# The order in which the first chunk's transfers are issued: next tiles of keys and values, weights and summaries in another sequence

## The chip, the cores and the metric

The kernel runs on one core of a Trainium2 chip. The metric is the device time of one execution in microseconds (us); the figure for the kernel before is the median of 3 runs. The trace comes from one further execution, taken by the hardware profiler. Its engines are TensorE (PE, with its weight loads as PEld), VectorE (DVE), ScalarE (ACT), GpSimd (POOL) and SyncE (SP); SP issues nearly all DMA transfers here.

## The reference

```
def _attn_ref(q, k, v):                      # batch 4, heads 8, sequence 768, head size 64
    block, window = (32, 16)
    k_sum = k.reshape(B, H, nb, block, D).max(axis=3)     # one maximum per 32 keys
    v_sum = v.reshape(B, H, nb, block, D).mean(axis=3)    # one mean per 32 values
    ...
    mask_l = np.abs(pos[:, None] - pos[None, :]) < window
    scores_s = scale * einsum(q, k_sum) + np.log(block)
    scores_all = np.concatenate([where(mask_l, scores_l, -1e9), scores_s], axis=-1)
    ...                                                   # softmax over both parts
    return np.matmul(a, np.concatenate([v, v_sum], axis=2))

def _moe_ref(x, w_in, w_out):                # x: 3072 x 512, w_in: 512 x 2048, w_out: 2048 x 512
    h = x @ w_in
    g = np.where(h > 0.0, h, exp(minimum(h, 0.0)) - 1.0)
    return g @ w_out
```

Each query attends to its neighbours in a window and to one summary per block of 32 (the maximum of the keys, the mean of the values). A feed-forward network with an ELU follows. The weights come as 64-bit floats.

## The kernel before

**Tiles.** The 3072 tokens are worked in 6 chunks of 512. In a chunk the network runs 16 steps, one for each 128 columns of the hidden layer: `layer1(c, f)` is 12 matmuls into a PSUM tile `h`, the ELU runs on ACT and DVE, `split` makes a high part `gh` (ACT) and a low part `gl` (POOL), and `layer2(c, f)` adds 12 matmuls into four accumulators one step later. Products are made in high and low parts, hence the pairs xh/xl and gh/gl.

**Attention beside it.** Attention for later tokens is cut into units: a third of a batch's sequence (256 queries) for one of four pairs of heads. Unit u is worked beside steps 2u and 2u+1. In step 2u TensorE makes the scores of unit u+1 (`unit_scores`, line 464), DVE finds their maxima (`unit_low`, line 130), ACT takes the exponentials, and TensorE makes the transposes of unit u (line 149); in step 2u+1 it makes the values of unit u (line 156), which ACT and DVE carry over to xh (line 169) and xl (line 170). The scores of unit u+1, the transposes and the values all use one PSUM bank, `a0`, in the first chunk.

**Loads of a unit.** `load_unit(u)` issues six transfers on SP (queries `qbd` in two, keys `kw` and values `vw` in a middle and an edge part): 64, 64, 144, 144, 40 and 40 KB.

**Summaries of the next batch.** `load_summary` brings 384 KB of keys or values of one pair of heads into a tile `n`, and `summary` reduces it on DVE (line 440). In the first chunk the tiles `n` lie in space that later belongs to weights (`spares`).

**Weights.** The 32 blocks of the two weight matrices, 512 KB each, come in the order (1,0), (1,1), (2,0), (1,2), (2,1), ..., where (1,f) is a block of w_in and (2,f) of w_out. `load_more(n)` issues loads until n blocks have been issued. `convert` turns a block into a high and a low part: POOL (line 103), ACT (108), DVE (110 and 113), ACT (117) and POOL (118). Two blocks are begun in every step of the first chunk, blocks number 4+2n and 5+2n in step n (counted from 0). The PSUM bank `a1` between ACT's line 108 and DVE's line 113 is one tile, so one conversion follows the other.

**Who sets the order.** The first chunk's instructions stand in the order in which the code is written, on all engines (`manual_schedule`); each engine works its queue in order. From the second chunk on only TensorE and SP are ordered by hand. Each DMA on SP also waits until the transfer eight before it has landed, since there are eight DMA semaphores in turn.

`first_units()` works the first 512 tokens' attention, converts the first blocks, and loads units 0 and 1; the loop `for n in range(NF)` with the 16 steps of the first chunk follows, and in each step `slot_a(n, 0)` makes unit scores and calls `load_unit(u + 2)` in even steps.

Of the kernel before, what the change touches and what calls it, by code (L numbers as in the profile page):

```python
# [17 lines left out]
F32 = mybir.dt.float32  # L18
# [8 lines left out]
P = 128  # L27
WIN = 16
E = WIN
BLK = 32  # L30
# [8 lines left out]
def attn_elu_ffn(ctx: ExitStack, tc: tile.TileContext, qT, kT, vT, v, w_in, w_out, out):  # L39
    nc = tc.nc  # L40
    B, NP, _, S = qT.shape
# [3 lines left out]
    NS = S // BLK  # L45
# [13 lines left out]
    att = ctx.enter_context(tc.tile_pool(name="att", bufs=2))  # L59
# [24 lines left out]
    def load(key):  # L84
        i, f = key
        if i == 1:
            load_weight(key, w_in[:, f * P:(f + 1) * P].rearrange("(c p) f -> p c f", p=P))
        else:
            load_weight(key, w_out[f * P:(f + 1) * P, :].rearrange("p (c f) -> p c f", c=1))

    def load_more(n):
        while loads and len(order) - len(loads) < n:
            load(loads.pop(0))
# [78 lines left out]
    def put_means(b, p, v_t, copy=None):  # L172
        src = vs_all[b][p * BLK:p * BLK + NS, :].rearrange("n (o d) -> n o d", o=1)
        (copy or nc.sync.dma_start)(out=v_t[KB:KC, :, :], in_=src.broadcast_to([NS, v_t.shape[1], P]))

    def put_maxima(b, p):
        nc.gpsimd.tensor_copy(out=kw[p][:, :, KB:KC], in_=ks_all[b][:, p:p + 1, :].broadcast_to([P, UW, NS]))

    def new_summaries(b):
        ks_all[b] = att.tile([P, NP, NS], F32, tag="ks", name="ks")  # L180
        vs_all[b] = att.tile([P, P], F32, tag="vs", name="vs", bufs=1)

    spares = {}

    def first_units():
# [74 lines left out]
        for p in range(NP):  # L260
            src = v[0, :, p * P:(p + 1) * P]
            whole = bass.AP(tensor=src.tensor, offset=src.offset + (QW - E) * row,
                            ap=[[row, KB], [QW * row, W2 - 1], [1, P]])
            nc.sync.dma_start(out=v_t[p][0:KB, 1:W2, :], in_=whole)
            nc.sync.dma_start(out=v_t[p][E:KB, 0, :], in_=src[0:KB - E, :])
        load_more(3)
        load_unit(0)
        load_more(6)
        load_unit(1)
        load_more(9)  # L270

        def maxima(p):
            nc.vector.tensor_reduce(out=ks[:, p, :], in_=kn[p][:, E:E + S].rearrange("p (n k) -> p n k", k=BLK),
# [107 lines left out]
        next(three)  # L381
        for p in range(NP):
            put_means(0, p, vw[p])
        load_more(12)
        return three


# [2 lines left out]
    def load_unit(u):  # L390
        third, p = units[u]
        b, th = divmod(third, NTH)
        q_t = qbd[u % 2]
        for h in range(2):
            nc.sync.dma_start(
                out=q_t[h * D:(h + 1) * D, :, h * D:(h + 1) * D],
                in_=qT[b, p, h * D:(h + 1) * D, th * UT:(th + 1) * UT].rearrange("d (t q) -> d t q", q=QW))
        lo = 1 if th == 0 else 0
        hi = UW - 1 if th == NTH - 1 else UW
        src = kT[b, p]  # L400
        nc.sync.dma_start(out=kw[p][:, lo:hi, 0:KB],
                          in_=bass.AP(tensor=src.tensor, offset=src.offset + (th * UW + lo) * QW - E,
                                      ap=[[S, P], [QW, hi - lo], [1, KB]]))
        vsrc = v[b, :, p * P:(p + 1) * P]
        nc.sync.dma_start(out=vw[p][0:KB, lo:hi, :],
                          in_=bass.AP(tensor=vsrc.tensor, offset=vsrc.offset + ((th * UW + lo) * QW - E) * row,
                                      ap=[[row, KB], [QW * row, hi - lo], [1, P]]))
        if th == 0:
            nc.sync.dma_start(out=kw[p][:, 0, E:KB], in_=src[:, 0:KB - E])
            nc.sync.dma_start(out=vw[p][E:KB, 0, :], in_=vsrc[0:KB - E, :])  # L410
            put_maxima(b, p)
        if th == NTH - 1:
            nc.sync.dma_start(out=kw[p][:, UW - 1, 0:KB - E], in_=src[:, S - KB + E:S])
            nc.sync.dma_start(out=vw[p][0:KB - E, UW - 1, :], in_=vsrc[S - KB + E:S, :])

    vst_all = {}

    def load_summary(b, p, src, spare=None):
        if p == 0 and src is kT:
            new_summaries(b)  # L420
            vst_all[b] = att.tile([P, NP, BLK], F32, tag="vst", name="vst", bufs=1)
            nc.gpsimd.memset(vst_all[b][:, :, NS:BLK], 0.0)
        parts = 1 if spare else 2
        m = NS // parts
        got = []
        for i in range(parts):
            if spare:
                n = wts.tile([P, m, BLK], F32, tag=spare, name="n")
            else:
                n = ffn.tile([P, m, BLK], F32, tag="cv", name="n", bufs=2)  # L430
            nc.sync.dma_start(out=n, in_=src[b, p, :, i * m * BLK:(i + 1) * m * BLK].rearrange("p (n k) -> p n k", k=BLK))
            got.append(n)
        return got

    def summary(b, p, src, got):

        dst, op = (ks_all[b], ALU.max) if src is kT else (vst_all[b], ALU.add)
        m = NS // len(got)
        for i, n in enumerate(got):
            nc.vector.tensor_reduce(out=dst[:, p, i * m:(i + 1) * m], in_=n, axis=AX.X, op=op)  # L440
# [32 lines left out]
    def unit_norm(u):  # L473
        normalize(sm_of[u], z_of.pop(u))
# [17 lines left out]
    def layer1(c, f):  # L492
        xh, xl = xs[c]
        w = weights[(1, f)]
        h_ps = psum.tile([P, CH], F32, tag="h", name="h", bufs=2)
        k = 0
        for cc in range(NCC):
            cols = slice(cc * P, (cc + 1) * P)
            for a, bb in ((0, xh), (0, xl), (1, xh)):
                nc.tensor.matmul(h_ps, w[:, a, cols], bb[:, cc, :], start=(k == 0), stop=(k == 3 * NCC - 1))  # L500
                k += 1
        return h_ps
# [78 lines left out]
    def begin_next():  # L581

        tile = convert() if todo else iter(())
        next(tile, None)
        return tile
# [4 lines left out]

    with tc.manual_schedule(engines=set(engines.values())):
        late = first_units()
        got = {}
        e = None
        this = begin_next()
        for n in range(NF):
            u, odd = divmod(n, 2)

            h_ps = layer1(0, n)
            next(this, None)  # L600
            ahead = begin_next()
            if n > 0:
                split(0, n - 1, e)
            next(this, None)
            if n > 0:
                evacuate()
            list(late)
            if not odd:
                unit_norm(u)
            for key in [(n - 1, 0), (n - 2, 1)]:  # L610
                if key in got:
                    summary(1, key[0], (kT, vT)[key[1]], got.pop(key))
            slot_a(n, 0)
            if n < NP:
                got[n, 0] = load_summary(1, n, kT, spares[0][n])
            if 1 <= n < NP + 1:
                got[n - 1, 1] = load_summary(1, n - 1, vT, spares[1][n - 1])
            load_more(12 + 3 * (n + 1))

            late, this = this, ahead  # L620
            next(this, None)
            ahead = begin_next()
            e = exp_of(h_ps)
            next(this, None)
            list(late)
            if not odd:
                low = unit_low(u + 1)
            elu(e, h_ps)
            if odd:
                unit_exps(u + 1, low)  # L630
            if n > 0:
                layer2(0, n - 1)
            late, this = this, ahead
            evacuate = slot_b(n, 0)
        list(late)
        split(0, NF - 1, e)
        evacuate()
        unit_norm(NF // 2)

    with tc.manual_schedule(engines={engines["PE"], engines["SP"]}):  # L640
        for n in range(NF, NCH * NF):
            c, f = divmod(n, NF)
            u, odd = divmod(n, 2)
            h_ps = layer1(c, f)
            e = exp_of(h_ps)
            turn = elu(e, h_ps)
            split(c, f, e)
            slot_a(n, c)
            if not odd and u + 1 < len(units):
                unit_exps(u + 1, unit_low(u + 1))  # L650
                unit_norm(u + 1)
            for b, first in first_of.items():
                p = n - (2 * first - 8)
                for q, src in ((p, kT), (p - 2, vT)):
                    if 0 <= q < NP:
                        got = load_summary(b, q, src)
                        with tc.issue_after(turn):
                            summary(b, q, src, got)
            layer2(*divmod(n - 1, NF))
            slot_b(n, c)()  # L660
        layer2(NCH - 1, NF - 1)
# [37 lines left out]
```

## Time and profile before

| what | value |
|---|---|
| median of 3 runs | 667.55 us (667.48 to 667.73) |
| the profiled execution | 666.64 us |
| its span, first to last instruction | 664.9 us |
| TensorE busy | 642.8 us, 97% of the span |
| VectorE, ScalarE, GpSimd busy | 265.3, 275.3, 244.1 us |
| DMA moved | 60.24 MB, mean 91 GB/s |

The span is the time from the first to the last instruction; the execution's own time holds 1.74 us more around it. Shares are means over the whole span, and the stages differ: DMA moves about 300 GB/s in the first sixth and little later. A row of a timeline gives start, duration, engine, line, operation and, in brackets, the idle time of the engine before it with what ended that.

### The profile page before, as it was taken

How to read it: one execution, taken by the hardware profiler on the slowest of the kernel's cores; microseconds unless marked ns; L12 is line 12 of the kernel's file. 1: busy time of each engine (PE TensorE's matmuls, PEld its weight loads, DVE VectorE, ACT ScalarE, POOL GpSimd, SP SyncE). 2: the span in 40 equal slices, each digit the busy share in tenths (PEclk: the TensorE clock that was granted, in tenths of full speed). 3: DMA queues.
4: the chain of work that ended last, by engine and by line, in shares of the span. 5: the costliest groups of instructions: out<-in, count | busy, mean ns of one | idle time of the engine just before them, and what ended most of it. 6: DMA issues, size and time to landing. Idle time of an engine off the chain costs nothing.

```text
span 664.9 us, 10778 instructions
## 1 busy us (share of the span) xinstructions
PE 642.8 (97%) x3916; PEld 525.1 (79%) x3916; DVE 265.3 (40%) x856; ACT 275.3 (41%) x750; POOL 244.1 (37%) x263
## 2 busy tenths in 40 slices
PE   8767899999999999999999999999999999999997
PEld 7655678888888887888888887888788888888885
DVE  7847877643323542323223452322332222322222
ACT  6754667653433344334333433433343333322222
POOL 5765789953232223222222322232223222222221
PEclk9977999999999999999999999999999999999999
DMA  9999981213132334112112552121312100100001
GB/s 317 253 287 328 333 260 42 67 33 96 39 79 57 112 92 118 51 32 60 36 32 55 162 142 52 44 62 33 96 40 53 32 1 1 63 1 1 0 1 63
DMA packets 86324, 60.24 MB, mean 91 GB/s; under 512 B 46464, under 2 KB 78464, under 8 KB 86272
## 3 DMA queue, kind: packets, MB, share of 16 engines
q1 hardware_dynamic: 82960, 53.66, 29.2%
q10 hardware_dynamic: 3312, 5.90, 2.4%
q8 instruction: 31, 0.51, 0.3%
q14 instruction: 21, 0.17, 0.1%
HBM read 52.46 MB, written 6.29 MB: 88 GB/s over the span
## 4 chain that ended last, share of the span: by engine, by line
PE 90%; DMA 6%; DVE 2%; SPq 1%; issue 1%; POOL 0%; ACT 0%; DVEq 0%; POOLq 0%
PE h L500 39%; PE o L528 38%; PE s L464 5%; PE o_ps L156 4%; DMA raw_w<-in_w_in_dram 3%; PE t_ps L149 3%; DMA raw_w<-in_w_out_dram 2%; PE s L287 1%; DMA vw<-in_v_dram 1%; DMA n<-in_vT_dram 1%; PE idle L224 1%; SPq L81 0%; DVE cv L113 0%; DVE sh L110 0%; DVE sm L130 0%
## 5 line engine op out<-in xcount | busy, mean ns | idle before, releaser
L500 PE MATMUL h<-xh,w 128*128 128x512 f32 x768 | 261.8, 402 | 0.0
L518 POOL TENSOR_TENSOR gl<-e,gh 128x512 fp32r<-128x512 f32 x96 | 123.5, 1287 | 217.4 <-issue 112.9
L528 PE MATMUL o<-w,gh 128*128 128x512 f32 x768 | 197.8, 396 | 0.0
L500 PEld LDWEIGHTS h<-xh,w 128*128 128x128 f32 x768 | 144.7, 189 | 31.0
L528 PEld LDWEIGHTS o<-w,gh 128*128 128x128 f32 x768 | 141.9, 189 | 28.6 <-issue 0.6
L500 PE MATMUL h<-xl,w 128*128 128x512 f32 x384 | 150.3, 391 | 0.0
L510 DVE TENSOR_SCALAR e<-e 128x512 f32<-128x512 f32 x96 | 43.7, 455 | 253.7 <-ACT e L506 253.6
L506 ACT ACTIVATE e<-h 128x512 f32<-128x512 f32 x96 | 57.3, 597 | 206.4 <-PE h L500 205.1
L144 POOL TENSOR_TENSOR sm<-sm,z 128x480 f32<-128x480 f32 x48 | 47.4, 987 | 158.1 <-ACT gh L517 141.9
L528 PE MATMUL o<-w,gl 128*128 128x512 f32 x384 | 105.4, 389 | 0.0
L517 ACT CAST gh<-e 128x512 fp32r<-128x512 f32 x96 | 59.0, 615 | 74.6 <-DVE e L511 73.3
L137 ACT ACTIVATE sm<-sm,mx 128x120 f32<-128x120 f32 x192 | 73.5, 385 | 26.6 <-DVE mx L130 26.6
L528 PEld LDWEIGHTS o<-w,gl 128*128 128x128 f32 x384 | 72.0, 188 | 15.2 <-POOL gl L518 0.2
L500 PEld LDWEIGHTS h<-xl,w 128*128 128x128 f32 x384 | 72.6, 189 | 12.8
L511 DVE SCALAR_TENSOR_TENSOR e<-h,e 128x512 f32<-128x512 f32 x96 | 66.2, 689 | 2.2
L464 PEld LDWEIGHTS s<-kw,qbd 128*128 128x128 f32 x320 | 43.1, 198 | 15.5 <-DVE xl L170 8.0
L464 PE MATMUL s<-kw,qbd 128*128 128x120 f32 x320 | 44.2, 283 | 11.2 <-DVE xl L170 6.7
L170 DVE TENSOR_TENSOR xl<-o_ps,xh 128x256 fp32r<-128x256 f32 x48 | 20.0, 422 | 61.3 <-ACT xh L169 61.3
L118 POOL TENSOR_TENSOR w<-cv,w 128x512 fp32r<-128x512 f32 x32 | 41.5, 1298 | 6.3 <-ACT w L117 5.5
L130 DVE CUSTOM_DVE_ANT_0 sm<-s,mask 128x120 f32<-128x120 f32 x192 | 42.2, 276 | 3.0 <-PE s L464 2.8
L137 ACT ACTIVATION_READ_ACCUMULATOR sm<-sm,mx 128x1 f32 x192 | 36.1, 188 | 0.0
L156 PEld LDWEIGHTS o_ps<-pt,vw 120*64 120x64 f32 x640 | 21.9, 137 | 14.1 <-ACT gh L517 9.2
(66 smaller groups left out, 369.3 us busy)
## 6 DMA issues: line engine op xcount, KB each, us to landing
raw_w<-in_w_in_dram SPq DMA_DIRECT2D x16, 512.0 KB, 4.5
raw_w<-in_w_out_dram SPq DMA_DIRECT2D x16, 512.0 KB, 9.4
qbd<-in_qT_dram SPq DMA_DIRECT2D x80, 64.0 KB, 2.3
out_dram<-ot ACTq DMA_DIRECT2D x20, 256.0 KB, 2.3
kw<-in_kT_dram SPq DMA_DIRECT2D x28, 144.0 KB
vw<-in_v_dram SPq DMA_DIRECT2D x28, 144.0 KB, 2.7
n<-in_kT_dram SPq DMA_DIRECT2D x16, 192.0 KB, 2.4
n<-in_vT_dram SPq DMA_DIRECT2D x16, 192.0 KB, 2.5
```

What stands on the lines that cost most here:

```text
L130: nc.vector.tensor_tensor_reduce(out=sm[:, t, :], in0=s_ps[:, t, :], in1=m, scale=-scale, scalar=3.0e38, op0=ALU.add, op1=ALU.min, accum_o ...
L137: nc.scalar.activation(out=sm[:, t, :], in_=sm[:, t, :], func=AF.Exp, bias=mx[:, t, :], scale=-1.0, accum_out=z[:, t, :])
L144: nc.gpsimd.tensor_tensor(out=sm, in0=sm, in1=z.broadcast_to([P, UW, KC]), op=ALU.mult)
L156: nc.tensor.matmul(o_ps[h * D:(h + 1) * D, t * QW:(t + 1) * QW], v_t[0:KC, w0 + t, h * D:(h + 1) * D], pt[0:KC, t, h * QW:(h + 1) * QW], s ...
L464: nc.tensor.matmul(s_of[u][:, t, :], qbd[u % 2][:, t, :], kw[p][:, t, :], start=True, stop=True)
L500: nc.tensor.matmul(h_ps, w[:, a, cols], bb[:, cc, :], start=(k == 0), stop=(k == 3 * NCC - 1))
L506: nc.scalar.activation(out=e, in_=h_ps, func=AF.Exp)
L510: nc.vector.tensor_scalar(out=e, in0=e, scalar1=1.0, scalar2=-1.0, op0=ALU.min, op1=ALU.add)
L511: top = nc.vector.scalar_tensor_tensor(out=e, in0=h_ps, scalar=0.0, in1=e, op0=ALU.max, op1=ALU.add)
L517: nc.scalar.copy(out=gh, in_=e)
L518: nc.gpsimd.tensor_tensor(out=gl, in0=e, in1=gh.bitcast(F32), op=ALU.subtract)
L528: nc.tensor.matmul(o_acc[c][s], a[:, s * P:(s + 1) * P], w[:, bb, :], start=first and f == 0, stop=last and f == NF - 1)
```

## The change

Three things are put in another order; no computation is added or taken away. In `first_units`, block (2,0) comes behind unit 0, and blocks (1,2) and (2,1) behind unit 1, where three blocks stood ahead of unit 0 and six ahead of unit 1; by the end of `first_units` 10 blocks are issued instead of 12. In step n the loads reach block count 12+2n instead of 12+3(n+1). The summaries follow a table `sums_at`: step number to a list of (0 for keys, 1 for values; pair of heads). A summary is loaded two steps before the step that reduces it, where it was loaded one step before (keys) or issued and reduced in neighbouring steps (values). New tiles for the summaries, and the memset of `vst`, move ahead of the loop.

```
-        load_more(3)
-        load_unit(0)
-        load_more(6)
+        load_more(2)
+        load_unit(0)
+        load_more(3)
         load_unit(1)
-        load_more(9)
+        load_more(5)
...
-        load_more(12)
+        load_more(10)
...
+        sums_at = {2: [(1, 0)], 3: [(0, 0)], 4: [(1, 1)], 5: [(0, 1), (1, 2)], 6: [(1, 3)], 7: [(0, 2)], 8: [(0, 3)]}
         got = {}
+        new_summaries(1)
...
-            for key in [(n - 1, 0), (n - 2, 1)]:
-                if key in got:
-                    summary(1, key[0], (kT, vT)[key[1]], got.pop(key))
+            for i, p in sums_at.get(n, []):
+                summary(1, p, (kT, vT)[i], got.pop((i, p)))
             slot_a(n, 0)
-            if n < NP:
-                got[n, 0] = load_summary(1, n, kT, spares[0][n])
-            if 1 <= n < NP + 1:
-                got[n - 1, 1] = load_summary(1, n - 1, vT, spares[1][n - 1])
-            load_more(12 + 3 * (n + 1))
+            for i, p in sums_at.get(n + 2, []):
+                got[i, p] = load_summary(1, p, (kT, vT)[i], spares[i][p])
+            load_more(12 + 2 * n)
```

On TensorE and ACT the sequence of instructions is the same before and after, and behind the first chunk it is the same on every engine. (A line that stands at 182 to 415 before stands 3 lines lower down in the change, and one from there to the loop stands 1 line higher up.)

SP, from the end of `first_units`, before: `raw_w_F_n<-in_w_in_dram` is block (1,F), `in_w_out_dram` block (2,F); `qbd_70`, `kw_72`, `vw_76` belong to unit 0 and `qbd_71`, `kw_73`, `vw_77` to unit 1.

```order
L81 DMA raw_w_0_181<-in_w_out_dram 128x512
L395 DMA qbd_70<-in_qT_dram 64x4x64 x2
L401 DMA kw_72<-in_kT_dram 128x3x96
L405 DMA vw_76<-in_v_dram 96x3x128
L413 DMA kw_72<-in_kT_dram 128x80
L414 DMA vw_76<-in_v_dram 80x128
L81 DMA raw_w_2_189<-in_w_in_dram 128x4x128
L81 DMA raw_w_1_191<-in_w_out_dram 128x512
L81 DMA raw_w_3_193<-in_w_in_dram 128x4x128
L395 DMA qbd_71<-in_qT_dram 64x4x64 x2
L401 DMA kw_73<-in_kT_dram 128x3x96
```

The same place of SP in the change:

```order
L398 DMA qbd_70<-in_qT_dram 64x4x64 x2
L404 DMA kw_72<-in_kT_dram 128x3x96
L408 DMA vw_76<-in_v_dram 96x3x128
L416 DMA kw_72<-in_kT_dram 128x80
L417 DMA vw_76<-in_v_dram 80x128
L81 DMA raw_w_0_187<-in_w_out_dram 128x512
L398 DMA qbd_71<-in_qT_dram 64x4x64 x2
L404 DMA kw_73<-in_kT_dram 128x3x96
L408 DMA vw_77<-in_v_dram 96x3x128
L416 DMA kw_73<-in_kT_dram 128x80
L417 DMA vw_77<-in_v_dram 80x128
L81 DMA raw_w_2_195<-in_w_in_dram 128x4x128
```

Block (2,0) moved behind unit 0, and blocks (1,2), (2,1) and (1,3) moved from ahead of unit 1 to behind it.

SP in steps 0 and 1, before, from the load of unit 2 (`qbd_70`, `kw_74`, `vw_78`) on; `n<-in_kT_dram` and `n<-in_vT_dram` are the summaries' loads:

```order
L395 DMA qbd_70<-in_qT_dram 64x4x64 x2
L401 DMA kw_74<-in_kT_dram 128x3x96
L405 DMA vw_78<-in_v_dram 96x3x128
L413 DMA kw_74<-in_kT_dram 128x80
L414 DMA vw_78<-in_v_dram 80x128
L431 DMA n<-in_kT_dram 128x768
L81 DMA raw_w_5_722<-in_w_out_dram 128x512
L81 DMA raw_w_7_724<-in_w_in_dram 128x4x128
L81 DMA raw_w_6_726<-in_w_out_dram 128x512
L431 DMA n<-in_kT_dram 128x768
L431 DMA n<-in_vT_dram 128x768
```

In the change:

```order
L398 DMA qbd_70<-in_qT_dram 64x4x64 x2
L404 DMA kw_74<-in_kT_dram 128x3x96
L408 DMA vw_78<-in_v_dram 96x3x128
L416 DMA kw_74<-in_kT_dram 128x80
L417 DMA vw_78<-in_v_dram 80x128
L430 DMA n<-in_vT_dram 128x768
L81 DMA raw_w_4_718<-in_w_out_dram 128x512
L81 DMA raw_w_6_720<-in_w_in_dram 128x4x128
L430 DMA n<-in_kT_dram 128x768
```

The first summary loaded is one of values, and 10 blocks of weights stand ahead of it where 12 stood ahead of the first one before; one summary follows a step where one to two did.

DVE in steps 1 and 2, before: lines 110 and 113 are a block's conversion, 440 a summary's reduction, 510 and 511 the ELU, 170 the values of unit 0.

```order
L110 SCALAR_TENSOR_TENSOR sh<-sh,raw_w_3_193 128x512
L113 SCALAR_TENSOR_TENSOR cv<-raw_w_3_193,sh 128x512
L440 TENSOR_REDUCE ks<-n 128x24
L110 SCALAR_TENSOR_TENSOR sh<-sh,raw_w_2_201 128x512
L113 SCALAR_TENSOR_TENSOR cv<-raw_w_2_201,sh 128x512
L510 TENSOR_SCALAR e<-e 128x512
L511 SCALAR_TENSOR_TENSOR e<-h,e 128x512
L110 SCALAR_TENSOR_TENSOR sh<-sh,raw_w_4_203 128x512
L113 SCALAR_TENSOR_TENSOR cv<-raw_w_4_203,sh 128x512
L170 TENSOR_TENSOR xl<-o_ps,xh 128x256
```

In the change:

```order
L110 SCALAR_TENSOR_TENSOR sh<-sh,raw_w_3_665 128x512
L113 SCALAR_TENSOR_TENSOR cv<-raw_w_3_665,sh 128x512
L110 SCALAR_TENSOR_TENSOR sh<-sh,raw_w_2_667 128x512
L113 SCALAR_TENSOR_TENSOR cv<-raw_w_2_667,sh 128x512
L509 TENSOR_SCALAR e<-e 128x512
L510 SCALAR_TENSOR_TENSOR e<-h,e 128x512
L110 SCALAR_TENSOR_TENSOR sh<-sh,raw_w_4_669 128x512
L113 SCALAR_TENSOR_TENSOR cv<-raw_w_4_669,sh 128x512
L170 TENSOR_TENSOR xl<-o_ps,xh 128x256
L142 TENSOR_SCALAR z<-z 128x4
L143 RECIPROCAL z<-z 128x4
L439 TENSOR_REDUCE vst<-n 128x24
```

No reduction stands in step 1 any more; the first one stands in step 2, behind the values of unit 0 (line 170).

## Rows read from the trace of the kernel before

**Rows 1.** The page, part 2: TensorE's clock and DMA over 40 slices of 16.6 us.

```profile
PEclk9977999999999999999999999999999999999999
DMA  9999981213132334112112552121312100100001
```

**Rows 2.** Stretches: PE, PEld, DVE, ACT, POOL busy, granted clock, DMA share, GB/s.

```profile
36.50:43.20 6.70, 4.86 (x17) 4.25 (x18) 5.04 (x15) 3.40 (x8) 4.50 (x6) 0.50 0.94 282
53.60:60.30 6.70, 4.08 (x14) 3.60 (x15) 5.74 (x11) 3.49 (x7) 4.97 (x5) 0.50 1.04 376
77.80:100.00 22.20, 22.20 (x135) 17.45 (x134) 16.58 (x35) 15.94 (x41) 18.21 (x20) 1.00 0.93 268
46.00:50.00 4.00, 4.00 (x32) 3.08 (x31) 0.00 (x0) 1.77 (x9) 1.96 (x2) 1.00 1.19 278
```

**Rows 3.** Who waited for whom, first 160 us: total, times, longest (us).

```profile
DVE ks L440 <- DMA n<-in_kT_dram: 10.8, 3, 8.0
PE s L464 <- DVE xl L170: 6.7, 3, 4.8
PE s L464 <- DMA kw<-in_kT_dram: 4.4, 1, 4.4
```

**Rows 4.** Timeline of TensorE, first chunk.

```profile
32.45 0.39 PE L500 MATMUL h<-xh,w 128*128 128x512 f32 x1
37.25 2.03 PE L464 MATMUL s<-kw,qbd 128*128 128x120 f32 x8 [4.42 <-DMA kw<-in_kT_dram]
40.37 1.08 PE L149 MATMUL t_ps<-ident,sm 128*120 128x128 f32 x4 [1.08 <-DVE mx L130]
...
48.37 0.50 PE L500 MATMUL h<-xh,w 128*128 128x512 f32 x1
...
56.22 2.06 PE L464 MATMUL s<-kw,qbd 128*128 128x120 f32 x8 [4.82 <-DVE xl L170]
...
62.24 0.47 PE L500 MATMUL h<-xh,w 128*128 128x512 f32 x1
...
68.50 0.50 PE L500 MATMUL h<-xh,w 128*128 128x512 f32 x1
...
77.39 0.63 PE L149 MATMUL t_ps<-ident,sm 128*120 128x128 f32 x4 [0.60 <-DVE mx L130]
77.77 0.47 PE L500 MATMUL h<-xh,w 128*128 128x512 f32 x1
...
84.05 0.50 PE L500 MATMUL h<-xh,w 128*128 128x512 f32 x1
...
91.06 0.47 PE L500 MATMUL h<-xh,w 128*128 128x512 f32 x1
```

**Rows 5.** Timeline of DVE, steps 0 to 2.

```profile
37.56 0.69 DVE L113 SCALAR_TENSOR_TENSOR cv<-raw_w,sh 128x512 uint32<-128x512 uint32 x1
39.32 0.28 DVE L130 CUSTOM_DVE_ANT_0 sm<-s,mask 128x120 f32<-128x120 f32 x1 [1.07 <-PE s L464]
...
42.30 0.69 DVE L113 SCALAR_TENSOR_TENSOR cv<-raw_w,sh 128x512 uint32<-128x512 uint32 x1
51.02 0.95 DVE L440 TENSOR_REDUCE ks<-n 128x24 f32<-128x768 f32 x1 [8.03 <-DMA n<-in_kT_dram]
```

**Rows 6.** POOL's first steps for blocks (1,2) with (2,1), then (1,3).

```profile
33.38 1.38 POOL L103 TENSOR_SCALAR raw_w<-raw_w 128x512 uint32<-128x512 uint8 x2
37.85 0.66 POOL L103 TENSOR_SCALAR raw_w<-raw_w 128x512 uint32<-128x512 uint8 x1
```

**Rows 7.** Timeline of SP: issue of block (1,2), and of the first blocks' means.

```profile
26.34 0.37 SPq L81 DMA_DIRECT2D raw_w<-in_w_in_dram  x1
...
36.62 3.51 SPq L174 DMA_DIRECT2D vw<-vs  x4
```

**Rows 8.** Line 81 at 26.3 us, block (1,2) alone: time from issue to landing.

```profile
DMA to landing us min/median/max: 4.4/4.4/4.4
```

**Rows 9.** The tile raw_w, all blocks: time from issue to landing.

```profile
DMA to landing us min/median/max: 4.4/6.5/10.0
```

More of the change, by code (lines that the diff above doesn't have):

```diff
@@ L181, in new_summaries @@
         vs_all[b] = att.tile([P, P], F32, tag="vs", name="vs", bufs=1)
+        if b > 0:
+            vst_all[b] = att.tile([P, NP, BLK], F32, tag="vst", name="vst", bufs=1)
+            nc.gpsimd.memset(vst_all[b][:, :, NS:BLK], 0.0)
     spares = {}
@@ L418, in load_summary @@
     def load_summary(b, p, src, spare=None):
[L419 to L422, printed above, removed]
         parts = 1 if spare else 2
@@ L653, in attn_elu_ffn @@
                 p = n - (2 * first - 8)
+                if p == 0:
+                    new_summaries(b)
                 for q, src in ((p, kT), (p - 2, vT)):
```

## The prediction

> **What bounds the kernel now.** I read the page's slices first. DMA is saturated only in the first six of 40 slices, and TensorE's granted clock falls below full only there [rows 1]; the stretches give that clock as 0.50 in 36.5 to 43.2 us and in 53.6 to 60.3 us, which is the lower level, 1.2 GHz [rows 2]. From 77.8 us on TensorE is busy without a gap [rows 2]: the rest of the kernel is bound by TensorE, whose sequence of instructions the change leaves as it is. So what it can give or cost lies between 30 and 78 us. The table of waits names the candidates there: DVE waited 8.0 us in one piece for the summary's keys, TensorE 4.8 us for DVE's xl and 4.4 us for a unit's keys [rows 3].
>
> The timeline of TensorE turns this into a loss per step. An undisturbed even step, from its first layer-1 matmul to that of the next step, takes 91.06 - 84.05 = 7.01 us, an undisturbed odd one 84.05 - 77.77 = 6.28 us [rows 4]. Step 2 took 62.24 - 48.37 = 13.87 us, step 3 took 6.26 us, step 4 took 77.77 - 68.50 = 9.27 us [rows 4]. Layer 1 of step 0 ended at 32.84 us, and TensorE then waited 4.42 us for unit 1's keys [rows 4].
>
> **Step 0: unit 1's keys come earlier, but DVE hides most of it.** Three blocks (1.57 MB) move from ahead of unit 1 to behind it. At 282 GB/s [rows 2] that is 5.6 us, so the keys that ended TensorE's wait at 37.25 us land at about 31.7 us, before 32.84, and the scores run at 32.84 to about 33.9. The next thing on TensorE, the transposes, needs the bank `a0` free of these scores, so it waits for DVE's maxima. DVE works them behind block (2,1)'s conversion, which ended at 37.56 + 0.69 = 38.25 us in a chain of conversions that goes POOL, ACT, DVE through the one bank `a1`; the maxima started at 39.32, only 1.07 us later [rows 5]. So of the 4.42 us the step keeps only **1.07 us**; the transposes start at 39.30 instead of 40.37 [rows 4].
>
> **Step 1: the clock.** From the transposes at 40.37 to layer 1 of step 2 at 48.37 it took 8.00 us; the same work undisturbed takes 84.05 - 77.39 = 6.66 us [rows 4]. The 1.34 us between are the half clock that held until about 43.2 us [rows 2]. In the change TensorE still idles from 33.9 to 39.3 us, and both half-clock stretches stand after such an idle time (from 32.84 and from about 51.4) [rows 2, 4]. I take the same stretch again, to 43.2: 3.9 us at half clock lose 1.95 us of work, so 6.66 + 1.95 = 8.61 us, **0.61 us worse** than before. Bounds: no fall at all, 6.66 us (1.34 better); or a fall only at the end of the idle time, at 39.3, that lasts as long as the two did (6.7 us), to 46.0: 3.35 us lost, 10.0 us, 2.0 us worse. The Trainium skill's page "TensorE: Matmul & The Clock Gate", section "Why this matters for your kernels", says the same against this change: a gap between bursts of matmuls drops the clock, whatever the gap was spent on. The trace agrees with its two stretches at 0.50.
>
> **Step 2: the summary that DVE stood on.** At 42.99 us (42.30 + 0.69) DVE had finished a block; it then stood until 51.02 for the first summary's keys [rows 5]. Behind it in DVE's queue were two conversions, the ELU of step 1 and xl of unit 0, and TensorE's scores of unit 2 waited 4.82 us for that xl [rows 4], with the second half-clock stretch behind that gap [rows 2]. The change takes the reduction out of step 1. Its first one stands in step 2, behind xl, with 10 blocks of weights ahead of its load instead of 12: 1.05 MB, 3.7 us at 282 GB/s, so it lands at about 47.3, where DVE reaches it at about 50 (layer 1 of step 2 at about 47.9, values done there, xl, z). The second one, keys, has 12 blocks and one summary (0.39 MB, 1.4 us) ahead: about 52.4, for a reduction in step 3, after 55. Neither is waited for, by 2 to 3 us. Step 2 becomes an undisturbed even step: 13.87 - 7.01 = **6.86 us gained**. If the load were late by more than the 2.7 us of margin, DVE's maxima of unit 2 would be late next, and with them TensorE's transposes.
>
> **Steps 3 to 8.** Step 3 was undisturbed (6.26 us). Step 4 lost 9.27 - 7.01 = 2.26 us, 0.60 of it in a wait for DVE's maxima just before the transposes [rows 4], DVE being behind with two summaries a step. In the change one reduction of 0.95 us [rows 5] stands in each step from 2 to 8, two in step 5, an odd step with no maxima. DVE then has, in the stretch from 77.8 us, 16.58 us busy of 22.20 [rows 2], 4.9 us a step of 6.55, so 5.8 with one reduction. It fits; I take the **2.26 us** as gained whole, with 0 to 2.26 as bounds.
>
> **What comes later for it.** Block (1,2) moves behind unit 1: it was issued at 26.34 [rows 7] and landed 4.4 us later [rows 8], at 30.7, while POOL took it only at 33.38 [rows 6]. A unit of 0.5 MB more ahead of it is 1.8 us at 278 GB/s, the stretch in which unit 2 landed [rows 2], and its own issue falls to about 29.9, behind six small ones; it lands at 32.5 to 34.3 us. POOL has other work until 33.3, and DVE wants it at 34.6, so I take zero; up to 1 us is open. Block (1,3) is now issued behind the four means, whose issue takes 3.51 us [rows 7]: at about 34.5 (29.9, a block more, the means), landing 4.4 us later, the shortest of all blocks [rows 9], at 38.9; POOL took it at 37.85 [rows 6], and DVE reaches it after the maxima and the ELU of step 0, at about 40.3. Zero again, with about 0.7 us of margin. From there on blocks are issued at least 6 ahead of those begun in a step (12+2n against 5+2n), three steps or 19.9 us, against a slowest landing of 10.0 us [rows 9]: hidden; without that cover each late microsecond would go to POOL's line 103 and the conversions. The memset of `vst` stands two conversions earlier on POOL, 0.12 us, hidden by the same margin. The number of transfers, reductions and conversions is the same, so nothing else costs.
>
> The Trainium skill's page "DMA: Bandwidth & Descriptors", section "Rules for kernel authors", speaks against putting units 0 and 1 nearly back to back: transfers under 64 KB are mostly overhead; its table gives 64 KB 138 GB/s, by which (an estimate) a unit would take 3.6 us, blocks would come 1.8 us later per unit and the sum would be about 3 us worse. The rows show 278 GB/s in the stretch of unit 2's six transfers and 282 in one of blocks and means [rows 2], so the sum goes without it.
>
> **The sum.** 1.07 - 0.61 + 6.86 + 2.26 = 9.58 us. The profiled execution took 666.64 us (span 664.9 and 1.74 around it); 666.64 - 9.58 = 657.1. The median of the runs stands 0.91 us above the profiled execution, so I expect a median of **658.0 us**, 1.4% less.
>
> **Rivals.**
> *The weights become the wait.* The burst of twelve small transfers and four means holds SP, and blocks (1,2) to (2,2) land 2 to 4 us later than I worked out. DVE's chain in steps 0 and 1 slips by that and TensorE idles longer at half clock. For it: my margins there are under 1 us. Against: DMA moved 278 to 282 GB/s with small transfers too [rows 2]. It gives 660 to 662.
> *The clock behaves otherwise.* If the scores of unit 1 at 33 to 34 us keep it up, step 1 is 1.95 us shorter: 656.0. If it is down until 46.0, 1.4 us longer: 659.4. For either: the two stretches began some 3.7 and 2.2 us after the idle time before them did (32.84 and 51.4) [rows 2, 4], so the moment is loose.
> *The gain is lost again.* The summaries land no earlier because DMA stays saturated, or DVE was in any case too full: step 2 keeps its wait. Against: DVE stood wholly idle for 8.03 us [rows 5], 0.00 busy in 46 to 50 us [rows 2]. It gives 666 to 667.5.
> *Slower: SP is held in step 7.* SP's transfer of the next batch's first means (line 174) waits there for TensorE and ACT. Before, no block was left behind it but now eight are, the first of them wanted in step 10, three steps or 19.9 us later. With a landing of up to 10.0 us [rows 9] the margin is 9.9 us. If SP were held longer, every microsecond would go to TensorE; it ends slower than before from about 20 us on, at 668 or more. Against: the means need only the summaries of values, reduced by step 6.
>
> **How the numbers follow.** My forecast 0.58, clock otherwise 0.18, weights late 0.15, gain lost 0.06, slower 0.03. The range reaches from the case without a fall, less 0.8 us for gains that I did not count (655.2), to late weights with their upper bound and the open 1 us (662.5); it leaves out about 0.15. A change of under 0.2%, 1.3 us, can hardly be told from none in this kernel: faster 0.93 (the first three and a part of the fourth), same 0.04, slower 0.03.
>
> **What would show it.** After the change, TensorE's scores of unit 1 at about 33 us without a wait for kw; its transposes at about 39.3, still waiting for DVE; one half-clock stretch instead of two; no wait of DVE for n over 1 us; layer 1 of step 2 at about 47.9, of step 3 at 54.9, of step 5 at 68.2 (77.77 before). Wrong if POOL's line 103 waits for raw_w by more than 1 us in steps 0 to 2, if DVE still waits for n, or if TensorE idles again in step 4.

## The result, and the profile after

The changed kernel takes **658.38 us** (median of 4 runs, 658.0 to 658.73) against 667.51 us on the same chip (median of 4); the ratio is 0.9865, with a 95% interval of 0.9847 to 0.9882. That is 9.13 us less. The profiled execution took 658.07 us, its span 656.3 us, which is 8.57 and 8.6 us less than before.

Part 2 of the page of the changed kernel answers to [rows 1]:

```profile
PEclk9969999999999999999999999999999999999999
DMA  9999965114122514121112551211321100100001
```

One slice with a low clock is left where there were two, and DMA's saturated stretch has given up its tail: the same bytes are moved later, beside work. The stretches of the changed kernel say how the clock stood (columns as in [rows 2]):

```profile
36.20:46.30 10.10, 5.97 (x16) 4.87 (x17) 7.43 (x20) 4.44 (x8) 8.74 (x9) 0.50 1.05 309
46.40:100.00 53.60, 53.60 (x317) 43.66 (x316) 44.40 (x99) 36.93 (x90) 45.52 (x47) 1.00 0.96 295
```

From 46.4 to 100 us TensorE is busy without a gap; before, it was so only from 77.8 us [rows 2]. The one stretch at half clock is longer than either of the two before. The timeline of TensorE answers to [rows 4]:

```profile
29.70 0.48 PE L499 MATMUL h<-xh,w 128*128 128x512 f32 x1
...
32.52 1.05 PE L463 MATMUL s<-kw,qbd 128*128 128x120 f32 x8
40.33 1.08 PE L149 MATMUL t_ps<-ident,sm 128*120 128x128 f32 x4 [6.76 <-DVE mx L130]
...
49.78 0.50 PE L499 MATMUL h<-xh,w 128*128 128x512 f32 x1
...
56.61 0.47 PE L499 MATMUL h<-xh,w 128*128 128x512 f32 x1
...
62.86 0.50 PE L499 MATMUL h<-xh,w 128*128 128x512 f32 x1
...
69.69 0.48 PE L499 MATMUL h<-xh,w 128*128 128x512 f32 x1
...
82.79 0.47 PE L499 MATMUL h<-xh,w 128*128 128x512 f32 x1
```

Unit 1's scores no longer wait. The transposes behind them start at 40.33 us all the same, after 6.76 us of idle time. In the kernel before, layer 1 of step 0 began at 29.84 us:

```profile
29.84 0.47 PE L500 MATMUL h<-xh,w 128*128 128x512 f32 x1
```

Step by step, in us:

| stretch of TensorE | before | predicted | after |
|---|---|---|---|
| transposes of step 0 start at | 40.37 | 39.30 | 40.33 |
| from there to layer 1 of step 2 | 8.00 | 8.61 | 9.45 |
| step 2 | 13.87 | 7.01 | 6.83 |
| step 3 | 6.26 | 6.26 | 6.25 |
| step 4 | 9.27 | 7.01 | 6.83 |
| steps 5 and 6 | 13.29 | 13.29 | 13.10 |

By the start of step 7 the change is ahead by 91.06 - 82.79 = 8.27 us, nearly all of the 8.6 us of the spans. Nearly the whole gain comes from steps 2 and 4 (9.48 us; steps 3, 5 and 6 give 0.20); steps 0 and 1 gave back 1.4 us. Timelines of DVE and POOL show why the transposes did not move:

```profile
35.70 0.70 DVE L110 SCALAR_TENSOR_TENSOR sh<-sh,raw_w 128x512 uint32<-128x512 uint32 x1 [1.89 <-POOL raw_w L103]
...
38.68 0.69 DVE L113 SCALAR_TENSOR_TENSOR cv<-raw_w,sh 128x512 uint32<-128x512 uint32 x1
39.29 0.28 DVE L130 CUSTOM_DVE_ANT_0 sm<-s,mask 128x120 f32<-128x120 f32 x1
...
51.82 0.92 DVE L439 TENSOR_REDUCE vst<-n 128x24 f32<-128x768 f32 x1
```

```profile
35.03 0.64 POOL L103 TENSOR_SCALAR raw_w<-raw_w 128x512 uint32<-128x512 uint8 x1 [1.81 <-DMA raw_w<-in_w_in_dram]
```

POOL waited 1.81 us for block (1,2), which now lands behind unit 1; DVE waited 1.89 us for POOL, and the maxima of unit 1 start at 39.29, where they started at 39.32 [rows 5]. A late block of weights took the place of the late keys. The first reduction, at 51.82, waited for nothing.

SP does stand in steps 6 and 7, ahead of the next batch's first means, with eight blocks behind it, as the rival for a slower kernel had it. Its own waits in the first 130 us show 8.4 us in one piece, and TensorE has no gap there:

```profile
SPq L174 <- ACT sh L108: 9.2, 2, 8.4
```

### The profile page after: what moved, and what is told of

Same layout as the page of the kernel before. It is cut to its first block, busy times and chain, and to the rows that moved or that the text cites. A ratio compares the mean times of both kernels' runs of the same rounds, so it can differ in the third digit from the quotient of the medians.

```text
span 656.3 us, 10774 instructions
## 1 busy us (share of the span) xinstructions
PE 639.7 (97%) x3916; PEld 523.8 (80%) x3916; DVE 265.7 (40%) x856; ACT 275.6 (42%) x750; POOL 245.3 (37%) x263
## 4 chain that ended last, share of the span: by engine, by line
PE 94%; DMA 2%; DVE 2%; ACT 1%; POOL 0%; SPq 0%; issue 0%; DVEq 0%
PE h L499 41%; PE o L527 40%; PE s L463 5%; PE o_ps L156 4%; PE t_ps L149 3%; DMA v<-in_v_dram 1%; DMA raw_w<-in_w_in_dram 1%; DMA raw_w<-in_w_out_dram 1%; DVE sm L130 1%; PE idle L227 1%; ACT sm L137 0%; PE s L290 0%; DVE sh L110 0%; DVE cv L113 0%; POOL raw_w L103 0%; DVE ks L276 0%
## 5 line engine op out<-in xcount | busy, mean ns | idle before, releaser
L509 DVE TENSOR_SCALAR e<-e 128x512 f32<-128x512 f32 x96 | 45.1, 469 | 254.2 <-ACT e L505 254.1
L144 POOL TENSOR_TENSOR sm<-sm,z 128x480 f32<-128x480 f32 x48 | 47.5, 990 | 157.0 <-ACT gh L516 130.9
L463 PE MATMUL s<-kw,qbd 128*128 128x120 f32 x320 | 41.9, 274 | 0.6 <-DVE xl L170 0.6
L149 PE MATMUL t_ps<-ident,sm 128*120 128x128 f32 x192 | 29.3, 276 | 8.5 <-DVE mx L130 6.8
```

The source lines that it names most:

```text
L144: nc.gpsimd.tensor_tensor(out=sm, in0=sm, in1=z.broadcast_to([P, UW, KC]), op=ALU.mult)
L149: nc.tensor.transpose(t_ps[0:KC, t, :], sm[:, t, :], ident)
L463: nc.tensor.matmul(s_of[u][:, t, :], qbd[u % 2][:, t, :], kw[p][:, t, :], start=True, stop=True)
L509: nc.vector.tensor_scalar(out=e, in0=e, scalar1=1.0, scalar2=-1.0, op0=ALU.min, op1=ALU.add)
```

## The experiments

My theory after the result: the gain is the reduction that DVE no longer stands on in step 1 (with the smoother steps behind it); the early units buy nothing, because DVE's conversions end step 0; and the gap that is left on TensorE costs its clock. The rival: the units' order carries part of the gain, or the earlier landing as such. Ratios are to the kernel before on the same chip (medians 667.45, 667.18 and 666.61 us in the three sets, 667.51 in the change's own), so versions of different sets are best compared by their ratios.

**The change with the old order of units.**

```
-        load_more(2)
-        load_unit(0)
         load_more(3)
+        load_unit(0)
+        load_more(6)
         load_unit(1)
-        load_more(5)
+        load_more(9)
...
-        load_more(10)
+        load_more(12)
```

> The change with the old order of the first transfers: three blocks ahead of unit 0, six ahead of unit 1, 12 by the end; summaries two steps early and 12+2n blocks kept. My theory: the gain is the summary that DVE no longer stands on; the early units buy nothing, since DVE's conversions end step 0. Then unit 1's scores are late again (at about 37.2 us) and the transposes start at about 40.3 as in both kernels; the half clock is the short one of the kernel before, step 2 starts at about 48.4 and step 3 at about 55.3, so about 657.0 us, 1.3 us below the change. Rival, the early units carry part of the gain: 660 us or more.

Measured: 657.96 us, ratio 0.986 [0.9843, 0.9878], the change's own time. TensorE's timeline:

```profile
30.71 0.47 PE L499 MATMUL h<-xh,w 128*128 128x512 f32 x1
...
38.23 2.04 PE L463 MATMUL s<-kw,qbd 128*128 128x120 f32 x8 [4.50 <-DVE sh L110]
41.34 1.08 PE L149 MATMUL t_ps<-ident,sm 128*120 128x128 f32 x4 [1.08 <-DVE mx L130]
...
50.64 0.50 PE L499 MATMUL h<-xh,w 128*128 128x512 f32 x1
...
57.48 0.47 PE L499 MATMUL h<-xh,w 128*128 128x512 f32 x1
```

The scores wait 4.50 us again, and it costs nothing: layer 1 of step 0 began at 30.71 us in this execution and at 29.70 in the change's, so the transposes start 10.63 us after it in both. (The bracket names DVE, but the same trace has the scores' keys landing at 37.98 us, 0.05 us before DVE's signal, so what ended the wait can't be told from it.) The early units, a good part of the diff, are worth nothing here. I had expected 1.3 us less than the change, from a short half clock as in the kernel before; in the profiled execution, the slowest of the four at 659.33 us, it was again the long one (0.50 from 36.9 to 46.9 us). The other three took 657.47 to 658.11 us; what their clock did is not shown.

**The kernel before with the new order of units alone.**

```
-        load_more(3)
-        load_unit(0)
-        load_more(6)
+        load_more(2)
+        load_unit(0)
+        load_more(3)
         load_unit(1)
-        load_more(9)
+        load_more(5)
```

> The kernel before with only the first transfers' order of the change (two blocks, unit 0, one block, unit 1, two blocks), and 12 blocks by the end as before. My theory: unit 1's scores run at about 33 us without a wait, but the transposes still wait for DVE until about 40.3, and DVE still stands until about 51 us for the first summary, so step 3 starts at about 62.2 as before: 667.0 to 668.0 us. Rival, the units' order carries the gain: 658 to 664 us.

Measured: 666.6 us, ratio 0.9991 [0.998, 1.0002]: no difference that can be told (the median lies 0.4 us under the range that I gave). Its table of waits still has the first row of [rows 3], 8.4 us now:

```profile
DVE ks L440 <- DMA n<-in_kT_dram: 10.2, 2, 8.4
```

The two experiments agree from both sides.

**The change with its first reduction in step 1.** SP's sequence is untouched; one instruction of DVE stands a step earlier.

```
-        sums_at = {2: [(1, 0)], 3: [(0, 0)], ...
+        sums_at = {1: [(1, 0)], 3: [(0, 0)], ...
...
-            for i, p in sums_at.get(n + 2, []):
+            for i, p in sums_at.get(n + 2 if n else 1, []):
```

> The change with its first summary reduced in step 1 instead of step 2; SP's sequence of transfers is that of the change. My theory: DVE stands again, from about 43 us until that summary lands at about 48.7, and the ELU and the conversions behind it come later by as much; step 3 starts about 1.8 us later than in the change or more: 660 to 661 us. Rival, what helped was the earlier landing and not the place in DVE's queue: 658.4 us.

Measured: 660.39 us, ratio 0.9896 [0.988, 0.9912], 2.0 us above the change. DVE's timeline, and then TensorE's:

```profile
43.44 0.70 DVE L113 SCALAR_TENSOR_TENSOR cv<-raw_w,sh 128x512 uint32<-128x512 uint32 x1
49.18 0.95 DVE L439 TENSOR_REDUCE vst<-n 128x24 f32<-128x768 f32 x1 [5.04 <-DMA n<-in_vT_dram]
...
53.91 0.42 DVE L170 TENSOR_TENSOR xl<-o_ps,xh 128x256 fp32r<-128x256 f32 x1
```

```profile
50.37 0.50 PE L499 MATMUL h<-xh,w 128*128 128x512 f32 x1
...
54.38 1.15 PE L463 MATMUL s<-kw,qbd 128*128 128x120 f32 x8 [0.99 <-DVE xl L170]
...
58.49 0.47 PE L499 MATMUL h<-xh,w 128*128 128x512 f32 x1
```

This is the wait of the kernel before in small: DVE stands 5.04 us, xl comes late behind it, TensorE waits 0.99 us for xl, and step 2 takes 8.12 us instead of 6.83. It stands for less time than the 8.03 of [rows 5], since the summary lands 1.84 us earlier and DVE comes to it 1.15 us later; no second half clock follows (1.00 from 47.5 to 60 us). So with the earlier landing alone step 2 is already 5.75 us shorter than the 13.87 of the kernel before. Of the 2.0 us, this trace shows 1.29 in step 2. The start of step 2 was already 0.59 us later than in the change (50.37 against 49.78) though TensorE had no gap in step 1: block (1,2), which the edit does not touch, came late in this execution (POOL took it at 36.26 us).

**The change with summaries loaded one step ahead.**

```
-            for i, p in sums_at.get(n + 2, []):
+            for i, p in sums_at.get(n + 1, []):
```

> The change with each summary loaded one step before its reduction instead of two; the table of reductions stays. The first one then takes the second one's place on SP, which landed at about 51.8 us in the change, just when DVE came to the first reduction. My theory: a wait of at most 1 us on DVE, inside its margin ahead of the transposes: 658.0 to 659.0 us. Rival, two steps early are needed: DVE waits in several steps and it takes 660 us or more.

Measured: 658.04 us, ratio 0.986 [0.9844, 0.9876]. From 40 us on DVE's waits for summaries are two short ones; the third row is the first reduction on DVE's timeline:

```profile
DVE ks L439 <- DMA n<-in_kT_dram: 0.6, 1, 0.6
DVE vst L439 <- DMA n<-in_vT_dram: 0.5, 1, 0.5
...
52.18 0.95 DVE L439 TENSOR_REDUCE vst<-n 128x24 f32<-128x768 f32 x1 [0.55 <-DMA n<-in_vT_dram]
```

They lie inside DVE's margin. Two steps early was not needed; a first reduction no earlier than step 2 was enough. The first summary landed at 52.18 us here, no earlier than the 51.02 of the kernel before [rows 5], and step 2 still takes 6.84 us. So the place in DVE's queue brings step 2's gain by itself, while the earlier landing by itself, in the run above, falls 1.29 us short of it.

**One block ahead of unit 1.**

```
-        load_more(3)
+        load_more(4)
         load_unit(1)
```

> The change with block (1,2) ahead of unit 1 instead of behind it. My theory: what kept the transposes of step 0 at 40.3 us is that this block landed at 35.0, 1.8 us after POOL was free for it; now DVE's chain runs as in the kernel before, unit 1 lands at about 34 and its scores still come before DVE is ready, and the transposes start at 39.3. 657.0 to 658.0 us, by how long the clock stays down. Rival, the lateness of the block is beside the point and another wait takes its place: transposes at 40.3 again, 658.4 us.

Measured: 657.91 us, ratio 0.9861 [0.9844, 0.9877]. My theory of it fell: the transposes started at 41.40, 11.52 us after the first layer 1. That the time lies in the range I gave all the same is luck: from the transposes to step 2 it took 8.47 us instead of 9.45, behind a shorter half clock. TensorE's timeline comes first; POOL's then has the wait at the next block, (2,1), which stayed behind unit 1:

```profile
41.40 1.08 PE L149 MATMUL t_ps<-ident,sm 128*120 128x128 f32 x4 [5.37 <-POOL raw_w L103]
```

```profile
33.48 0.65 POOL L103 TENSOR_SCALAR raw_w<-raw_w 128x512 uint32<-128x512 uint8 x1
37.73 0.64 POOL L103 TENSOR_SCALAR raw_w<-raw_w 128x512 uint32<-128x512 uint8 x1 [3.60 <-DMA raw_w<-in_w_out_dram]
```

**All three blocks ahead of unit 1.**

```
-        load_more(3)
-        load_unit(1)
         load_more(5)
+        load_unit(1)
```

> The change with all three blocks (2,0), (1,2) and (2,1) between unit 0 and unit 1. With block (1,2) alone ahead, the wait moved to block (2,1). My theory: DVE's chain in step 0 wants the blocks before unit 1, whose scores have time until 38 us; now no block is late, unit 1 lands at about 36 and the transposes of step 0 start 9.5 us after the first layer 1 instead of 10.6. 657.0 to 658.1 us, by how long the clock stays down. Rival, the bytes come too late in any order and the wait moves to unit 1: transposes 10.5 us or more after, 658.4 us.

Measured: 656.96 us, ratio 0.9845 [0.9829, 0.9862]. TensorE's timeline:

```profile
35.49 1.12 PE L462 MATMUL s<-kw,qbd 128*128 128x120 f32 x8 [2.60 <-DMA kw<-in_kT_dram]
39.28 1.08 PE L149 MATMUL t_ps<-ident,sm 128*120 128x128 f32 x4 [2.67 <-DVE mx L130]
...
47.85 0.50 PE L498 MATMUL h<-xh,w 128*128 128x512 f32 x1
```

Now the transposes start at 39.28, 9.38 us after the first layer 1 (29.90). So the 39.30 that I had predicted was to be had, by letting unit 1 be later: its scores wait 2.60 us, and that is hidden under DVE. From there to step 2 it took 8.57 us, behind a half clock of the short kind (0.50 from 36.7 to 43.3 us), where I had predicted 8.61: with no block late, steps 0 and 1 come out as worked out.

**Matmuls whose result nobody reads, in TensorE's gap.** The edit adds work that the output does not depend on.

```
             slot_a(n, 0)
+            if n == 0:
+                fill_ps = psum.tile([P, CH], F32, tag="o0", name="fill")
+                for k in range(24):
+                    nc.tensor.matmul(fill_ps, weights[(1, 0)][:, 0, k % NCC * P:(k % NCC + 1) * P],
+                                     xs[0][0][:, k % NCC, :], start=True, stop=True)
```

> The change with 24 matmuls more on TensorE behind unit 1's scores in step 0, whose result nobody reads, to keep TensorE busy until about 39 us while it waits for DVE. My theory: the half clock that stood from 36.1 to 46.4 us in the change does not come, the transposes still start at about 40.3, and step 1 takes 6.7 us from there instead of 9.45: 655.6 us. Rival, step 1 is paced by DVE and ACT rather than by the clock: 657.5 to 658.5 us.

Measured: 657.37 us, ratio 0.9853 [0.9834, 0.9872]. The stretches, and TensorE's timeline:

```profile
33.00:41.90 8.90, 6.49 (x33) 5.17 (x31) 5.25 (x17) 4.65 (x13) 4.68 (x7) 1.00 0.91 282
```

```profile
41.97 0.62 PE L149 MATMUL t_ps<-ident,sm 128*120 128x128 f32 x4 [2.48 <-POOL raw_w L103]
...
48.60 0.50 PE L499 MATMUL h<-xh,w 128*128 128x512 f32 x1
```

The clock stays at 1.00, and from the transposes to step 2 it takes 48.60 - 41.97 = 6.63 us instead of 9.45: the theory of the clock holds to 0.1 us. The median lies 1.0 us under the change's and not 2.8 (the runs spread from 655.82 to 658.72 us, so the 1.0 is not clear of noise): block (1,2) came later still in the profiled execution, and the transposes with it, 11.92 us after the first layer 1. Whether that is the filling's doing is not settled. POOL took that block at 35.0 to 36.3 us in the four executions with the same first transfers and no filling, at 36.6 here, where SP's issue of it alone took 1.96 us instead of 0.43; the next run, with another order of blocks, shows no delay.

**Three blocks ahead and 11 such matmuls before and 11 behind unit 1's scores.**

Against the version with three blocks ahead:

```
+        def fill(count):
...
+            if n == 0:
+                fill(11)
             slot_a(n, 0)
+            if n == 0:
+                fill(11)
```

> The same with 11 matmuls more on TensorE ahead of unit 1's scores and 11 behind them, whose result nobody reads. My theory: no half clock, transposes 9.5 us after the first layer 1 and step 1 of 6.7 us behind them: 654.6 us. Rival, the wait moved to unit 1, or the added matmuls slow the transfers: 656 to 657.5 us, as with the filling alone.

Measured: 656.18 us, ratio 0.9841 [0.9823, 0.9858], 1.6 us short of what I expected. The transposes came 9.38 us after the first layer 1, as without the filling, and from there to step 2 it took 6.63 us; but step 2 then took 7.44 us, and POOL had waited 1.98 us for block (1,3). The next late thing is that block, behind the four means on SP.

**Blocks (1,3) and (2,2) ahead of the means, without and with the filling.**

Against the same version; the second run has the matmuls of the last one too:

```
         load_unit(1)
+        load_more(7)
```

> The change with three blocks between units 0 and 1, and blocks (1,3) and (2,2) moved ahead of the four means on SP. My theory: in the version with three blocks alone POOL waited 2.7 us for block (1,3), but TensorE was then paced by the half clock and not by that; so DVE and POOL run earlier and the time stays, 656.5 to 657.2 us. Rival, the block was what paced step 1: 655.5 us or less.

Measured: 656.73 us, ratio 0.985 [0.983, 0.987]: no gain while the half clock paces step 1, as expected.

> The same with the 11 and 11 matmuls whose result nobody reads. My theory: without the half clock block (1,3) did pace DVE and POOL, which cost step 2 0.6 us (7.44 instead of 6.84 us); with it earlier step 2 takes 6.85 us: 655.3 us. Rival, POOL's own work paces step 2: 656.2 us as before.

Measured: **655.09 us**, ratio 0.9824 [0.9804, 0.9844], the fastest version: 3.3 us below the change's median, 2.7 us by the ratios (0.9824 against 0.9865). TensorE's timeline:

```profile
32.75 2.65 PE L600 MATMUL fill<-xh,w 128*128 128x512 f32 x11
36.05 1.34 PE L463 MATMUL s<-kw,qbd 128*128 128x120 f32 x8 [0.65 <-DMA kw<-in_kT_dram]
37.15 2.79 PE L600 MATMUL fill<-xh,w 128*128 128x512 f32 x11
39.77 0.60 PE L149 MATMUL t_ps<-ident,sm 128*120 128x128 f32 x4
40.13 0.48 PE L499 MATMUL h<-xh,w 128*128 128x512 f32 x1
...
46.39 0.50 PE L499 MATMUL h<-xh,w 128*128 128x512 f32 x1
...
53.52 0.48 PE L499 MATMUL h<-xh,w 128*128 128x512 f32 x1
```

Step 2 takes 7.13 us: half of the 0.6 us is regained, where I had expected all of it. The transposes follow the filling without a gap, so here it may even have held them up by a few tenths.

## Why the prediction was right

The time, 658.0 forecast and 658.38 measured, and the main mechanism were right; two terms of the sum were mis-sized, both to the same side. Worked out on the profiled executions, 9.58 us were forecast and 8.57 came: 1.87 us too much in steps 0 and 1, 0.86 too little in the rest. The medians lie 0.56 us further apart than the two profiled executions, which hid half of what was missing. So the mechanism of steps 2 and 4 was right, but that the time came within 0.4 us is in part luck.

*Step 0, 1.07 us: it came to 0.04,* and to nothing behind layer 1 of step 0 (10.53 us before, 10.63 after). DVE did end the step, as I said, and the early keys were hidden under it. But I took "zero; up to 1 us is open" for block (1,2), which I had landing at 32.5 to 34.3 us; POOL took it at 35.03. That is the rival of the late weights in small, and its sign came: I had called the prediction wrong if POOL's line 103 waited for raw_w by more than 1 us in steps 0 to 2, and it waited 1.81 us. The step that failed is the landing of a block behind twelve small transfers: a block issued only at 30.4 us, with unit 1 still to move, comes 4.6 us later. The run with three blocks ahead of unit 1 shows it: the term is there once no block is late (with one block ahead, the next one was late). The times that I gave for the transposes and for layer 1 of steps 2, 3 and 5 were missed, by 1.0 to 1.9 us, with this term and the next.

*Step 1, 0.61 us lost: it was 1.45.* The clock fell as forecast, behind the idle time that was left; the stretch was 10.1 us and not 6.7. It lies inside the bounds that I gave (2.0 us). The filling shows that the whole of it is the clock.

*Step 2, 6.86 us: it was 7.04*, and *step 4, 2.26 us: it was 2.44.* DVE did not wait for summaries, xl came in time, and no second half clock followed. Both are 0.18 more because the even steps now take 6.83 us, less than the 7.01 that I took as undisturbed. The reduction put back into step 1 brought DVE's stand back and cost 2.0 us, 1.29 of them in step 2. The first summary's landing was put too early: I had 47.3 us, and where DVE waited for it behind the same transfers it landed at 49.18. The margin covered that.

*Costed at nothing.* Fewer blocks ahead from step 1 on, the memset and SP's stand in steps 6 and 7 cost nothing that the profile shows. The sum also took the small transfers to move as fast as blocks, from a stretch of 278 GB/s [rows 2] that held a part of unit 2 beside blocks and a summary. Units 0 and 1 went out between 20 and 32 us, and there it was not so (the kernel before, the change, and the change with three blocks ahead of unit 1):

```profile
20.00:32.00 12.00, 10.02 (x162) 8.40 (x163) 9.93 (x27) 7.63 (x20) 8.12 (x9) 1.00 0.98 256
20.00:32.00 12.00, 10.12 (x162) 8.48 (x163) 9.80 (x27) 7.63 (x19) 8.12 (x10) 1.00 0.93 210
20.00:32.00 12.00, 9.97 (x161) 8.39 (x162) 9.94 (x27) 7.63 (x20) 8.18 (x9) 1.00 0.93 255
```

With the units nearly back to back DMA moved 46 GB/s less for 12 us, 0.55 MB or about one block. All five runs with the change's first transfers have 205 to 210 GB/s there, the seven with more blocks between the units 227 to 267. Whether the rate fell by the size of the transfers or because only eight are in flight at a time is not shown.

The prediction's estimate by the Trainium skill's page "DMA: Bandwidth & Descriptors" (64 KB at 138 GB/s, section "Bandwidth"; coalesce small transfers, section "Rules for kernel authors") was 3 us lost. The trace agrees with its direction and not with its size: 210 GB/s, and about 1 us lost in step 0.

*The range.* Its upper end, 662.5 us, does not follow from the terms named for it (662 and 1 us make 663); nothing rests on it here.

## What to carry to other kernels

Where an engine works its queue in order, the costly thing about a late transfer is what stands behind the instruction that waits for it; put that instruction behind the work others wait for, and the transfer may be just as late. A transfer that ended a wait is worth moving only if nothing else ends the same step a moment later: look at what the next engine in the chain was doing when the data came. While DMA is saturated, bringing one transfer forward makes another late, so give the early places to what is wanted first, and let that be later which has cover.

## What the runs showed of the hardware

The half clock behind nearly the same idle gap lasted differently long. Behind 4.42 us in the kernel before it stood for 6.7 us [rows 2], behind 4.50 us with the old units for 10.0; behind 6.76 us in the change for 10.1, behind 6.95 us in the version that loads one step ahead for 6.6 (0.50 from 38.0 to 44.6 us). I cannot say what decides it; it is worth about 1 us (9.45 us from the transposes to step 2 in the change, 8.32 in the version that loads one step ahead), and one pair of profiles is not to be read finer than that. Twenty-two matmuls of about 0.24 us each in the gap kept the clock at 1.00 from 30 to 100 us and bought 1.6 us net (656.73 to 655.09). A summary that lands at 51.02 or 52.18 us costs 8.03 us of DVE's time or 0.55 us by where its reduction stands in DVE's queue. From 20 to 32 us, while twelve transfers of 40 to 144 KB went out with one block between the two units, DMA moved 205 to 210 GB/s in five runs; with two or three blocks between the units it moved 227 to 267 GB/s in seven.
